# An early expert's list, gathers and weights: ranks moved ahead of the value products, all weight loads moved behind the gathers

## The chip, the cores and the metric

One core of one Trainium2 chip runs the whole program in one launch. The metric is the device time of one execution in microseconds (us), the median of three timed runs. One further execution was taken by the hardware profiler.

## The reference

The first stage is linear attention with a decay per head, for 4 batches, 8 heads, 768 positions and 64 columns a head; its output is the input of the second stage, a mixture of 8 experts in which each of the 3072 tokens goes to one expert.

```python
for b in range(nb):                               # blocks along the sequence
    intra = einsum(qb, kb) * Dmask                # decayed scores in the block
    out[:, :, sl] = intra @ vb + (qb * lam_pow) @ kv_state
    kv_state = lam_block * kv_state + (kb * rev_pow).T @ vb

x = out.transpose(0, 2, 1, 3).reshape(B * S, H * D)   # 3072 tokens x 512
logits = x @ w_gate                                    # 512 x 8
expert_idx = argmax(logits, axis=1)
gate_w = softmax(logits)[arange(N), expert_idx]
for e in range(8):
    mask = expert_idx == e
    out[mask] = gate_w[mask, None] * (maximum(x[mask] @ w1[e], 0) @ w2[e])   # 512->1024->512
```

## The kernel before

**Attention in steps.** The sequence is cut into six blocks of 128 positions (`n` = 0 to 5), and each block into two pairs of batches, which gives twelve steps. A step `i` of the loop works on three things at once: it makes the output rows and the router's logits of the step before (`leave`), it turns queries and keys of the step after (`enter`), and it computes the current step's state products (`attend_states`), the new state (`grow`) and the value products (`attend`). The scores of the next step (`score`) come last.

**Routing.** When the logits of a group of tokens are there, VectorE chooses each token's expert (`choose`). TensorE then computes the token's rank on its expert's list by products with triangular and full matrices of ones (`ranks`, tile `rank`), ScalarE copies it, and VectorE turns it into a place (`put`, tiles `place`, `slot`, `slot_i`). GpSimd writes one entry a token to that place in `slots`, in device memory, with an indirect DMA (`store_places`, line 467). The token rows themselves are stored to `xs` by ScalarE's queue (line 386).

**An early part of one expert.** Expert 5 (`FIRST`) does not wait for all tokens. Once the tokens of the first four blocks are placed (the group named `early`, ranked in loop step 8), the first 256 entries of its list are read (`start_early`, `list_0a`, line 497), its token rows are gathered on GpSimd (`gather_early`, tile `xg`, line 528), and its weights w1 and w2 (2 MB each) are loaded on SyncE's queue. After the last attention step TensorE turns the gathered rows (`tp`) and computes the hidden values (`ph`, line 607). For the output VectorE makes sums over w2 (`t_q`, `t_v`, `t_k`, `t_m`, line 684) and over the hidden values (`h_sd`, `h_qT`, `h_kT`, `h_kd`), from which seven products replace eight (line 775).

**Order.** `pin` keeps instructions of an engine in the order of the code; the rest is placed by a scheduler. A queue is worked off in order: an instruction that waits holds up what stands behind it on its engine. An explicit dependency (`add_manual_dep`, `hold`) makes one instruction wait for another's end. Before the change the first gather waits for the last scores of the step (`hold(begun[0], other)`), one half of w1 (by its rows) is loaded after the last attention inputs, the other half waits for the early list, and w2 waits for the gathers.

Of the kernel before, what the change touches and what calls it, by code (L numbers as in the profile page):

```python
# [22 lines left out]
def kernel(  # L23
# [207 lines left out]
    def pin(inst):  # L231
        tc.keep_in_program_order(inst)
        return inst
# [813 lines left out]
    def store_places(most, pin=pin):  # L1047
        put = None
        for k in range(min(most, len(waiting))):
            group, store, j = waiting.pop(0)  # L1050
            if k > 0:

                pin(nc.gpsimd.memset(between, 0.0))
            put = store(j)
            pin(put)
            if group[:2] == early and j == 1:
                start_early()
        return put

    def hold(inst, other):  # L1060
# [61 lines left out]
    def load_early():  # L1122

        w1t = wpool.tile([P, DC, F], F32, tag="w1", name="w1t")
        w2t = wpool.tile([P, FC, MD], F32, tag="w2", name="w2t")
        pin(nc.sync.dma_start(out=w1t[:, :DC // 2], in_=w1_r[FIRST][:, :DC // 2]))
        weights.append((w1t, w2t))

    def load_rest():

        rest = pin(nc.sync.dma_start(out=weights[0][0][:, DC // 2:], in_=w1_r[FIRST][:, DC // 2:]))
        tc.add_manual_dep(rest.ins, passes[0].read.ins.name, mybir.DependencyInfo(
            mybir.DependencyClass.Sync, mybir.DependencyReason.DATA),
            reason="the early list has the DMA engines first")

    def start_early():

        nc.vector.tensor_scalar(out=skip, in0=had, scalar1=-1.0, scalar2=float(EARLY),
                                op0=ALU.mult, op1=ALU.add)
        nc.vector.tensor_scalar_max(skip, skip, 0.0)  # L1140
        base[0] = const.tile([P, E], F32, name="ebase_late")
        nc.vector.tensor_copy(base[0], ebase)
        nc.vector.tensor_add(base[0][:, FIRST:FIRST + 1], base[0][:, FIRST:FIRST + 1], skip)
        passes.append(make_pass(FIRST, 0, EARLY, "0a", pin, nc.gpsimd))
        load_rest()

    def gather_early(other):

        m, w2t = passes[0], weights[0][1]
        pin(nc.gpsimd.memset(between, 0.0))  # L1150
        begun = fetch(m, 1 + (NSTEP - 2) * B * C, pin)
        hold(begun[0], other)
        behind = nc.sync.dma_start(out=w2t, in_=w2_r[FIRST])
        pin(behind)
        for other in begun:
            tc.add_manual_dep(behind.ins, other.ins.name, mybir.DependencyInfo(
                mybir.DependencyClass.Sync, mybir.DependencyReason.DATA),
                reason="the gathers have the DMA engines first")

    with tc.issue_after(keys_made.ins):  # L1160
        later_decays()
# [36 lines left out]
    fade(ahead)  # L1198
    last, cur = one, ahead

    for i in range(2, len(steps)):
        rest = leave(last, (4, 6, 7) if i < len(steps) - 1 else (4, 2, 3))

# [7 lines left out]
        if cur.n < NSTEP - 1:  # L1211
            attend_states(cur)
            grow(cur)
            attend(cur)
        else:
            attend(cur)
            attend_states(cur)
        to_sbuf(cur)
        if cur.n == NSTEP - 1:
            if ahead:  # L1220
                for s in range(2):
                    score(ahead, s)
                gather_early(ahead.scored)
            else:
                rest()
        update(cur)
# [6 lines left out]
        for group in ranked:  # L1233
            give_places(group)
        if ahead and i < len(steps) - 3:
            fade(ahead)
            store_places(1 if i < 5 else 2)
        last, cur = cur, ahead
    def turn_early():
        with tc.issue_after(decided[-1].ins):  # L1240
# [176 lines left out]
```

## Time and profile before

| | us |
|---|---|
| median of 3 timed runs | 433.21 (433.08 to 433.89) |
| the profiled execution's own time | 430.65 |
| its span | 428.9 |
| TensorE busy | 418.3 |
| VectorE, ScalarE, GpSimd busy | 263.5, 175.8, 256.8 |

The span is the time from the first to the last instruction in the trace; all times of day below are counted from its start. Busy time is time in which an engine works on an instruction; a wait that the profile names is idle time of an engine, put down to what ended it.

### The profile page before, as it was taken

To read this page: it belongs to the slowest core of one execution; us is meant where nothing else is said; L and a number is where in the kernel's file an instruction comes from. 1 tells how busy PE (TensorE), PEld (TensorE's weight loads), DVE (VectorE), ACT (ScalarE), POOL (GpSimd) and SP (SyncE) were. 2 spreads that over 40 slices of the span, in tenths; PEclk is the share of its full clock that TensorE was granted. 3 is DMA by queue.
4 is the path that set the end of the run, shared out by engine and by line. 5 is a ranking of instruction groups with operands and counts; after the bars stand their busy time and mean duration, and the time that the engine had idled before them with its cause. 6 is when DMAs were issued, how large, how long until landed. Compare 5 with 4: busy or idle time off the path is not lost. (4 is left out here: it accounts for less than half of the span.)

```text
span 428.9 us, 9593 instructions
## 1 busy us (share of the span) xinstructions
PE 418.3 (98%) x3707; PEld 393.1 (92%) x3707; DVE 263.5 (61%) x586; ACT 175.8 (41%) x318; POOL 256.8 (60%) x204
## 2 busy tenths in 40 slices
PE   8999999999999999999999999999999999999993
PEld 7878989888878897999999999999999999999973
DVE  7556646777567437686557657555565565765463
ACT  3365456556441434350654244345323605422221
POOL 4242556472444366977857848793884897749033
PEclk9999999999999999999999999999999999999998
DMA  9999999999985749975478746975975794753121
GB/s 173 209 247 239 210 245 237 229 228 222 284 287 165 224 93 272 282 262 213 64 162 224 281 74 150 311 200 126 292 240 79 218 373 74 156 188 55 21 82 63
DMA packets 164551, 83.11 MB, mean 194 GB/s; under 512 B 145923, under 2 KB 145959, under 8 KB 164496
## 3 DMA queue, kind: packets, MB, share of 16 engines
q1 hardware_dynamic: 155024, 63.21, 60.9%
q0 software_dynamic: 5536, 12.88, 9.4%
q10 hardware_dynamic: 3936, 6.31, 4.1%
q8 instruction: 31, 0.51, 0.5%
q14 instruction: 24, 0.20, 0.1%
HBM read 58.96 MB, written 12.72 MB: 167 GB/s over the span
## 5 line engine op out<-in xcount | busy, mean ns | idle before, releaser
L534 POOL DMA_INDIRECT out_dram<-o_room,list x24 | 26.3, 1097 | 53.3 <-DMA decay<-planes_q 29.4
L286 DVE TENSOR_TENSOR mt<-sp,decay 128x512 f32<-128x512 f32 x48 | 30.0, 684 | 19.8 <-PE sp L279 19.8
L740 ACT ACTIVATE hT<-hT 128x418 f32<-128x418 f32 (+6 forms) x56 | 28.1, 520 | 32.5 <-DVE hT L737 31.4
L729 PE MATMUL p<-xgT,w1t 128*128 128x209 f32 (+6 forms) x224 | 41.4, 327 | 0.0
L729 PEld LDWEIGHTS p<-xgT,w1t 128*128 128x128 f32 x224 | 37.1, 190 | 0.8 <-issue 0.8
L619 ACT COPY u_qT<-p 128x418 f32<-128x418 f32 (+6 forms) x14 | 6.7, 479 | 68.7 <-PE p L729 68.7
L915 PE MATMUL p<-hT,w2t 128*128 128x209 f32 (+5 forms) x192 | 33.6, 328 | 0.0
L915 PEld LDWEIGHTS p<-hT,w2t 128*128 128x128 f32 x192 | 32.0, 190 | 0.0
L528 POOL DMA_INDIRECT xg<-xs,list x25 | 26.1, 1044 | 9.1 <-issue 5.8
L467 POOL DMA_INDIRECT slots<-entry,slot_i x24 | 23.8, 990 | 12.2 <-PE tl L391 6.1
L737 DVE TENSOR_TENSOR hT<-p,u_kd 128x418 f32<-128x418 f32 (+6 forms) x28 | 15.6, 559 | 20.4 <-PE p L729 20.4
L279 PE MATMUL sp<-qT,kT 64*128 64x128 f32 x384 | 25.6, 280 | 0.6 <-DVE qs_room L255 0.6
L269 POOL TENSOR_TENSOR kd<-k_in,kdec 128x512 f32<-128x512 f32 x12 | 12.5, 1050 | 22.2 <-issue 10.7
L656 POOL TENSOR_TENSOR s_q<-w1t 128x1024 f32<-128x1024 f32 x7 | 16.5, 2361 | 14.9 <-DVE t_xT L714 12.9
L279 PEld LDWEIGHTS sp<-qT,kT 64*128 64x128 f32 x384 | 22.7, 188 | 2.8 <-issue 1.9
L607 PE MATMUL ph<-xgT,w1t 128*128 128x256 f32 (+1 forms) x128 | 21.6, 329 | 0.0
L326 ACT COPY xT<-op 128x512 f32<-128x512 f32 x12 | 7.0, 585 | 35.0 <-PE op L314 30.6
L586 ACT COPY xgT<-decay 128x1672 uint16<-128x1672 uint16 (+6 forms) x7 | 13.6, 1940 | 18.7 <-DMA decay<-planes_k 11.0
L607 PEld LDWEIGHTS ph<-xgT,w1t 128*128 128x128 f32 x128 | 19.3, 191 | 1.8 <-DVE xgT L598 0.3
L958 ACT ACTIVATE o_room<-o_room,list 128x512 f32<-128x512 f32 (+6 forms) x22 | 14.1, 709 | 16.1 <-DMA o_room<-qs_room 16.1
L729 PE MATMUL p<-t_sd,w1t 128*128 128x209 f32 (+6 forms) x112 | 20.7, 327 | 0.0
L729 PE MATMUL p<-st,s_q 128*128 128x209 f32 (+6 forms) x112 | 20.7, 327 | 0.0
(253 smaller groups left out, 1100.7 us busy)
## 6 DMA issues: line engine op xcount, KB each, us to landing
w2t<-in_moe_w_dram SPq DMA_DIRECT2D x8, 2048.0 KB, 9.4
w1t<-in_moe_w_dram SPq DMA_DIRECT2D x7, 2048.0 KB, 15.7
xs<-x_room ACTq DMA_DIRECT2D x12, 512.0 KB, 5.7
v_in<-in_v_dram SPq DMA_DIRECT2D x8, 512.0 KB, 8.8
o_room<-qs_room SPq DMA_DIRECT2D x76, 48.0 KB, 2.1
q_in<-in_q_dram SPq DMA_DIRECT2D x7, 512.0 KB, 8.8
k_in<-in_k_dram SPq DMA_DIRECT2D x7, 512.0 KB, 7.8
room<-in_q_dram SPq DMA_DIRECT2D x4, 512.0 KB, 9.1
```

The costliest lines, as they stand in the source:

```text
L279: m.scored = pin(nc.tensor.matmul(sp[u][:, i, b, :], lhsT=m.kT[s][halves[u], i, b, :], rhs=m.qT[s][halves[u], i, b, :], start=(i == 0 and ...
L286: nc.vector.tensor_mul(mt[:, u], sp[u], decay[:, u, s * HP // 2:(s + 1) * HP // 2].unsqueeze(2).to_broadcast(shp))
L467: put = nc.gpsimd.indirect_dma_start(out=slots, out_offset=bass.IndirectOffsetOnAxis(ap=slot_i[:, i:i + 1], axis=0), in_=entry[:, n, bs[i] ...
L528: return nc.gpsimd.indirect_dma_start(out=dst, out_offset=None, in_=xs[:rows, :], in_offset=bass.IndirectOffsetOnAxis(ap=idx, axis=0))
L534: put = nc.gpsimd.indirect_dma_start(out=out, out_offset=bass.IndirectOffsetOnAxis(ap=idx, axis=0), in_=src, in_offset=None, bounds_check= ...
L607: nc.tensor.matmul(ph, lhsT=w1t[:, dc, fc * P:(fc + 1) * P], rhs=m.xgT[:, dc, :], start=(dc == 0), stop=(dc == DC - 1))
L656: return nc.gpsimd.tensor_tensor(out=o, in0=x, in1=y, op=ALU.subtract)
L729: nc.tensor.matmul(p[:, i, :], lhsT=lhs[:, dc, g, i * P:(i + 1) * P], rhs=rhs[:, dc, :], start=(dc == 0), stop=(dc == DH - 1))
L737: lambda i, k, p, u: nc.vector.tensor_add(outs[i][k], p, u),
L740: pin(nc.scalar.activation(outs[i][k], outs[i][k], ACT.Relu))
L915: nc.tensor.matmul(p[:, c, :], lhsT=lhs[:, f, c * P:(c + 1) * P], rhs=rhs[:, f, :], start=(f == 0), stop=(f == FC // 2 - 1))
L958: pin(nc.scalar.activation(o_room[:w, t], o_room[:w, t], ACT.Copy, scale=gate))
```

## The change

The early group's ranks (on TensorE) and places (on VectorE) are issued in loop step 8 between `grow` and `attend`, and its two stores ahead of `fade`, the product `sd` on GpSimd; the list is read behind `fade`. The first gather no longer waits for the scores. The early part of w1 ahead of the list and its rest behind it are gone: w1, now in two column parts of 512 hidden columns each, and w2 are issued together, all three behind both gathers.

```diff
-            if group[:2] == early and j == 1:
-                start_early()
...
         w1t = wpool.tile([P, DC, F], F32, tag="w1", name="w1t")
         w2t = wpool.tile([P, FC, MD], F32, tag="w2", name="w2t")
-        pin(nc.sync.dma_start(out=w1t[:, :DC // 2], in_=w1_r[FIRST][:, :DC // 2]))
         weights.append((w1t, w2t))
-
-    def load_rest():
-
-        rest = pin(nc.sync.dma_start(out=weights[0][0][:, DC // 2:], in_=w1_r[FIRST][:, DC // 2:]))
-        tc.add_manual_dep(rest.ins, passes[0].read.ins.name, mybir.DependencyInfo(
-            mybir.DependencyClass.Sync, mybir.DependencyReason.DATA),
-            reason="the early list has the DMA engines first")
...
         passes.append(make_pass(FIRST, 0, EARLY, "0a", pin, nc.gpsimd))
-        load_rest()
-
-    def gather_early(other):
-
-        m, w2t = passes[0], weights[0][1]
+
+    def gather_early():
+
+        m, (w1t, w2t) = passes[0], weights[0]
         pin(nc.gpsimd.memset(between, 0.0))
         begun = fetch(m, 1 + (NSTEP - 2) * B * C, pin)
-        hold(begun[0], other)
-        behind = nc.sync.dma_start(out=w2t, in_=w2_r[FIRST])
-        pin(behind)
-        for other in begun:
-            tc.add_manual_dep(behind.ins, other.ins.name, mybir.DependencyInfo(
-                mybir.DependencyClass.Sync, mybir.DependencyReason.DATA),
-                reason="the gathers have the DMA engines first")
+        f = F // 2
+
+        for to, of in ((w1t[:, :, :f], w1_r[FIRST][:, :, :f]), (w1t[:, :, f:], w1_r[FIRST][:, :, f:]),
+                       (w2t, w2_r[FIRST])):
+            behind = pin(nc.sync.dma_start(out=to, in_=of))
+            for other in begun:
+                tc.add_manual_dep(behind.ins, other.ins.name, mybir.DependencyInfo(
+                    mybir.DependencyClass.Sync, mybir.DependencyReason.DATA),
+                    reason="the gathers have the DMA engines first")
...
         if cur.n < NSTEP - 1:
             attend_states(cur)
             grow(cur)
+            if chosen and chosen[-1][:2] == early:
+
+                for group in give_ranks():
+                    give_places(group)
+                last_early = i
             attend(cur)
...
-                gather_early(ahead.scored)
+                gather_early()
...
         if ahead and i < len(steps) - 3:
+            if i == last_early:
+                store_places(2)
             fade(ahead)
-            store_places(1 if i < 5 else 2)
+            if i == last_early:
+                start_early()
+            else:
+                store_places(1 if i < 5 else 2)
```

On TensorE, in loop step 8, before the change: the early group's ranks (`rank`) stand between the two halves of the next step's scores (`sp`).

```order
L279 MATMUL sp_1663<-qT,kT 128x128
L441 LDWEIGHTS before
L441 MATMUL rank<-oh,before 128x24
L441 LDWEIGHTS ones
L441 MATMUL rank<-so_far,ones 128x24
L441 LDWEIGHTS ones
L441 MATMUL rank<-oh,ones 128x16
L441 LDWEIGHTS ones
L441 MATMUL rank<-oh,ones 128x8
L279 MATMUL sp_1682<-qT,kT 128x128
```

And in the changed kernel, on TensorE in the same step: the ranks stand between the new state's products (`cp`) and the value products (`op`).

```order
L340 MATMUL cp<-room_68,kd 64x64 x16
L441 LDWEIGHTS before
L441 MATMUL rank<-oh,before 128x24
L441 LDWEIGHTS ones
L441 MATMUL rank<-so_far,ones 128x24
L441 LDWEIGHTS ones
L441 MATMUL rank<-oh,ones 128x16
L441 LDWEIGHTS ones
L441 MATMUL rank<-oh,ones 128x8
L314 MATMUL op_1605<-mt,room_68 64x128 x2
```

The same eight instructions moved up past the value products and half of the scores. VectorE follows: its places and `slot_i` stand ahead of the four `mt` products of that step instead of between and behind them.

On GpSimd, at the end of the same step (`kd` is the decayed keys of the step after, `sd` the faded state, `list_0a` the early list):

```order
 L269 TENSOR_TENSOR kd<-room_69,kdec 128x512
-L352 TENSOR_TENSOR sd<-st,sdec 128x512
-L467 DMA slots<-entry,slot_i 27648x4
-L1053 MEMSET between 128x1
-L467 DMA slots<-entry,slot_i 27648x4
+L467 DMA slots<-entry,slot_i 27648x4
+L1053 MEMSET between 128x1
+L467 DMA slots<-entry,slot_i 27648x4
+L352 TENSOR_TENSOR sd<-st,sdec 128x512
 L497 DMA list_0a<-slots 128x2x4
```

The two stores moved ahead of `sd`; the list read stays behind all three. Behind it stand, as before, two stores of the next group and then the two gathers.

On SyncE's queue, from the last attention inputs (`v_in`) to the first list of the later stage (`turns` is read for its expert):

```order
 L116 DMA v_in<-in_v_dram 128x16x64 x2
-L1126 DMA w1t<-in_moe_w_dram 128x2x1024
-L1131 DMA w1t<-in_moe_w_dram 128x2x1024
-L1153 DMA w2t<-in_moe_w_dram 128x8x512
-L1289 TENSOR_LOAD turns
+L1145 DMA w1t<-in_moe_w_dram 128x4x512 x2
+L1145 DMA w2t<-in_moe_w_dram 128x8x512
+L1291 TENSOR_LOAD turns
```

There are three loads of the same bytes in the same places of the queue; what each waits for and which part of w1 it brings is different.

## Rows read from the trace of the kernel before

**Rows 1.** The page's first line, and its line of busy times (us, share of the span, instructions).

```profile
span 428.9 us, 9593 instructions
PE 418.3 (98%) x3707; PEld 393.1 (92%) x3707; DVE 263.5 (61%) x586; ACT 175.8 (41%) x318; POOL 256.8 (60%) x204
```

**Rows 2.** All waits of TensorE between 85 and 165 us: who waited for whom, us in total, times, longest.

```profile
PE p L783 <- DVE u_t L820: 0.4, 1, 0.4
PE tx L376 <- ACT xT L326: 0.3, 1, 0.3
```

**Rows 3.** Timelines of TensorE and VectorE around the early part of the expert: start, duration, engine, line, operation, out<-in, count, in brackets idle time before it and what ended it.

```profile
122.07 2.00 PE L607 MATMUL ph<-xgT,w1t 128*128 128x256 f32 x8
139.63 1.89 PE L775 MATMUL p<-t_k,h_kT 128*128 128x256 f32 x8
...
131.16 1.23 DVE L684 TENSOR_TENSOR t_q<-w2t 128x1024 f32<-128x1024 f32 x1 [3.50 <-DMA w2t<-in_moe_w_dram]
136.79 0.69 DVE L754 TENSOR_TENSOR h_qT<-hT 128x512 f32<-128x512 f32 x1 [0.27 <-ACT hT L560]
137.52 0.69 DVE L755 TENSOR_TENSOR h_kT<-h_qT,hT 128x512 f32<-128x512 f32 x1
```

**Rows 4.** Timeline of TensorE: the scores and the logits behind them in a step without ranks, and in the step with the early group's ranks between the halves of the scores.

```profile
73.56 2.06 PE L279 MATMUL sp<-qT,kT 64*128 64x128 f32 x32
75.54 0.64 PE L366 MATMUL lgT<-xT,gates 128*32 128x256 f32 x8
...
92.89 1.16 PE L279 MATMUL sp<-qT,kT 64*128 64x128 f32 x16
...
95.27 0.64 PE L366 MATMUL lgT<-xT,gates 128*32 128x256 f32 x8
```

**Rows 5.** Timeline of VectorE: state updates (`st`), `mt` products and the two `slot_i` in question, the early group's and the next group's.

```profile
91.33 0.69 DVE L362 TENSOR_TENSOR st<-cp,sd 128x512 f32<-128x512 f32 x1 [0.24 <-PE cp L340]
94.09 1.29 DVE L286 TENSOR_TENSOR mt<-sp,decay 128x512 f32<-128x512 f32 x2 [2.06 <-PE sp L279]
...
98.01 0.16 DVE L465 CAST slot_i<-slot 128x2 int32<-128x2 f32 x1
...
101.12 0.69 DVE L362 TENSOR_TENSOR st<-cp,sd 128x512 f32<-128x512 f32 x1
...
106.95 0.17 DVE L465 CAST slot_i<-slot 128x2 int32<-128x2 f32 x1
```

**Rows 6.** Timeline of GpSimd: `sd`, the early group's two stores, the list read and the two gathers.

```profile
95.33 1.04 POOL L352 TENSOR_TENSOR sd<-st,sdec 128x512 f32<-128x512 f32 x1
98.45 1.00 POOL L467 DMA_INDIRECT slots<-entry,slot_i  x1 [2.08 <-DVE lg L393]
...
99.76 0.96 POOL L467 DMA_INDIRECT slots<-entry,slot_i  x1 [0.19 <-issue]
107.11 0.78 POOL L497 DMA_DIRECT2D list_0a<-slots  x1 [6.39 <-DMA slots<-entry,slot_i]
...
113.89 1.00 POOL L528 DMA_INDIRECT xg<-xs,list_0a  x1 [3.31 <-PE rank L441]
115.19 0.97 POOL L528 DMA_INDIRECT xg<-xs,list_0a  x1 [0.30 <-issue]
```

**Rows 7.** Timeline of SyncE's queue: the rest of w1 and w2 of the early expert, and a later expert's w2 and w1.

```profile
111.52 0.37 SPq L1131 DMA_DIRECT2D w1t<-in_moe_w_dram  x1
119.75 0.37 SPq L1153 DMA_DIRECT2D w2t<-in_moe_w_dram  x1
...
184.16 0.38 SPq L204 DMA_DIRECT2D w2t<-in_moe_w_dram  x1
184.79 0.37 SPq L202 DMA_DIRECT2D w1t<-in_moe_w_dram  x1
```

**Rows 8.** Issue to landing of transfers. First two lines of the page (count, size of each, median us to landing): the two halves of the early w1, and the row stores. Then the landing lines of the views of one tile: w1 between 95 and 140 us (two halves and the next expert's 2 MB), w2 in the same stretch (one load), w1 between 180 and 205 us (one load, that issued at 184.79).

```profile
w1t<-in_moe_w_dram SPq DMA_DIRECT2D x2, 1024.0 KB, 6.7
xs<-x_room ACTq DMA_DIRECT2D x12, 512.0 KB, 5.7
DMA to landing us min/median/max: 6.7/8.0/9.2
DMA to landing us min/median/max: 11.3/11.3/11.3
DMA to landing us min/median/max: 13.7/13.7/13.7
```

**Rows 9.** Stretches of two microseconds: length, busy time of TensorE, its weight loads, VectorE, ScalarE, GpSimd (instructions), granted clock, busy share of the DMA engines, GB/s moved.

```profile
122.00:124.00 2.00, 1.98 (x13) 1.63 (x13) 1.68 (x13) 0.85 (x3) 1.48 (x3) 1.00 0.95 334
124.00:126.00 2.00, 2.00 (x14) 1.80 (x12) 1.84 (x18) 0.56 (x2) 1.80 (x4) 1.00 0.94 251
126.00:128.00 2.00, 2.00 (x11) 1.74 (x11) 1.45 (x9) 0.64 (x2) 1.50 (x2) 1.00 1.05 407
```

**Rows 10.** The rows of the expert behind the early one: the last transpose for `decay` on SyncE's queue, the page's line of such transposes (median us to landing), ScalarE's copy that joins them, and TensorE's wait for `u_t`.

```profile
152.04 1.19 SPq L578 DMA_TRANSPOSE decay<-planes_k  x1
decay<-planes_k SPq DMA_TRANSPOSE x11, 3.5
156.09 2.09 ACT L586 COPY xgT<-decay 128x1672 uint16<-128x1672 uint16 x1 [7.72 <-PE ph L607]
163.03 1.08 PE L783 MATMUL p<-w2t,qs_room 128*64 128x256 f32 x8 [0.36 <-DVE u_t L820]
```

More of the change, by code (lines that the diff above doesn't have):

```diff
@@ L1199 @@
     last, cur = one, ahead
+    last_early = None
     for i in range(2, len(steps)):
```

## Prediction

> **What bounds the kernel now.** I read the page's first lines, then the waits of TensorE, then the timelines of every engine between 88 and 165 us, and last the transfers. TensorE is busy 418.3 of the 428.9 us, and almost none of what is left is waiting: between 85 and 165 us, where the whole change lies, it waits 0.4 us for VectorE's `u_t` and 0.3 us for ScalarE's `xT` [rows 1, 2]. So the reader should see two things. An earlier list, gather or weight can take away a wait of TensorE only if there is one, and there is 0.7 us of it. A later weight can make a new one without limit. The question is therefore how much slack each moved thing had, and how much it keeps.
>
> The slack before. The early hidden products start at 122.07, and the first half of w1 and its rest are there by then. The sums over w2 start on VectorE the moment w2 lands, at 131.16; VectorE has 0.27 us of rest before `h_qT`, and `h_kT`, finished at 138.21, is read by TensorE at 139.63, 1.42 us later [rows 3]. So w2 may land 0.27 + 1.42 = 1.7 us later, at 132.8, before TensorE notices.
>
> **The change part by part.**
>
> *The early ranks go ahead of the step's value products.* They are the same four products on TensorE. Between two halves of the scores they cost something: from the scores to the logits it is 75.54 - 73.56 = 1.98 us without ranks, and 95.27 - 92.89 = 2.38 us with them, 0.40 us [rows 4]. Their new place, between two other groups, may cost as much (gain 0) or nothing (gain 0.4). I take a gain of 0.2 us. The products they need from VectorE (`oh`) are ready before the state update at 91.33, so they wait for nothing new.
>
> *VectorE computes the places ahead of the `mt` products.* `slot_i` was ready at 98.17, behind them. Now the chain starts behind the update that ends at 92.0, in the 2.06 us in which VectorE was idle until 94.09; four to five small operations of about 0.2 us put `slot_i` at about 93.2 [rows 5]. The cost on the path is nothing: that idle time hides it, and were it too short, `mt` would be some tenths late, with TensorE reading it a whole set of products later.
>
> *On GpSimd the two stores pass the `sd` product.* The first takes the start of `sd`, about 95.5 instead of 98.45, the second 96.8 instead of 99.76. `sd` (1.04 us) comes 2.6 us later and ends near 99; its reader, the next state update, stands at 101.12, so this costs nothing with 2 us of cover, and beyond them one for one [rows 5, 6]. The list read waited for the second store until 107.11, 7.35 us after that store's start; the same wait now gives 104.2. The list then lands 4.4 us later, as before between 107.11 and the load at 111.52 that waited for it: 108.6 [rows 6, 7].
>
> *The gathers are no longer held for the scores.* They were released at 113.89. What stands ahead of them now is the pair of stores of the next group, whose `slot_i` is made at 106.95 to 107.12 and does not move. Stores and gathers follow each other at 1.3 us: stores at 107.3 and 108.6, gathers at 109.9 and 111.2 instead of 113.89 and 115.19 [rows 5, 6]. The list (108.6) is there. So the gathers gain 4.0 us, not the whole lead of the list. Behind them on GpSimd stand stores that wait for later ranks anyway.
>
> *All of w1 and w2 wait for both gathers.* The load of w2 was issued 119.75 - 115.19 = 4.56 us after the second gather started [rows 6, 7]; so the three loads are now issued at 111.2 + 4.6 = 115.8. For w2 that is 4 us earlier; for the rest of w1 (111.52) it is 4.3 us later, and for its early part far later still. Behind them in SyncE's queue stand only the lists of the later experts, which wait for the last routing anyway, so it is the weights alone that wait.
>
> First column part, 1 MB: the rest of w1, also 1 MB and also beside half a megabyte of other traffic, took 6.7 us to land; 115.8 + 6.7 = 122.5 against the use at 122.07, a stall of 0.4 us [rows 3, 8]. Bounds: no stall if the gathers land half a microsecond sooner, and with the 9.2 us of the slowest w1 load in that stretch 125.0, a stall of 2.9 us. The Trainium skill ("DMA: Bandwidth & Descriptors", section on the anatomy of one DMA on the gpsimd path) fits a transfer by about 2.0 us plus its bytes over 436 GB/s. An estimate from it is 4.4 us for this part, which would land at 120.2 and stall nothing, and the sum would end at 433.0. This case's trace does not agree: 6.7 us for 1 MB, 11.3 us for 2 MB.
>
> Second column part: first needed by the fifth of eight hidden blocks; the row at 122.07 is one block, 2.00 us, so four of them hide it for 7 to 8 us, more than the whole 6.7 us of such a load [rows 3, 8].
>
> w2 is now last of 4 MB in one queue. Lower bound: the pair w2 and w1 of a later expert, issued at 184.16 and 184.79, had landed 13.7 us after the second issue, 14.3 us after the first: 115.8 + 14.3 = 130.1. Upper bound: twice the 11.3 us that w2 took here, 22.6 us: 138.4, a stall of 5.6 us [rows 7, 8]. In between: 4.2 MB of weights and two row stores of 0.52 MB are 5.2 MB; at the mean of 122 to 128, (334 + 251 + 407) / 3 = 331 GB/s, that is 15.8 us, landing at 131.6 [rows 8, 9]. I take 131.6, nearer the pair because the bytes lie behind each other in one queue as they do there: about when it lands today, with 1.2 us of slack left.
>
> **Sum.** -0.2 (ranks) + 0.4 (first part of w1) + 0 (w2, places, `sd`, second part) = +0.2 us. The profiled execution took 430.65 us, 428.9 of span and 1.75 around it; 430.9 after. The median of the timed runs, 433.21, is 2.56 us above the profiled one; with the same difference, 433.4 us. A measurement of this kernel can tell about 0.2% (0.87 us) from no change, so this is no change.
>
> **Rivals.**
>
> *Slower: the weights are late.* The point from which it decides is w2 at 133.7 or the first part of w1 at 122.9. For it: the rate between 124 and 126 is only 251 GB/s [rows 9], and both slacks left are near one microsecond. Against it: the later pair, which landed in 14.3 us [rows 7, 8]. Landing one to two microseconds past these points costs as much: 434.4 to 435.4; at the upper bound of w2 438.8.
>
> *The early stores land no earlier, so the change doesn't do what it says.* If the list read stays at 107.11 because the input loads, not the store's start, set its landing, the list lands at 111.5, the gathers start at 111.6 and 112.9, the loads at 117.5, w1's first part lands at 124.2: stall 2.1 us, 435.1. For it: the second store took 7.35 us although it moves 2 KB [rows 6].
>
> *The later lists are late.* The last stores run beside w2. The transposes of the next expert's rows, last one for `decay` issued at 152.04, must land before 156.09, where ScalarE's join stands behind TensorE; at 3.5 us from issue to landing they have 0.5 us of slack, and what comes later reaches TensorE through `u_t`, where it waits already (0.36 us) [rows 10]. Two microseconds late gives 434.7. Against it: the DMA engines carry the same bytes by 130 us as before.
>
> *Faster.* All of it must come together: 0.4 us from the ranks and both waits of 0.7 us gone, 1.1 us in all, 432.1. For it: w2 may land 1 us sooner, and the list chain with it. Against it: neither wait is for a transfer or a list directly [rows 2].
>
> **How the numbers follow.** Forecast (-0.4 to +0.8 us about no change) 0.56; weights late 0.17; stores no earlier 0.07; lists late 0.06; faster 0.14. Predicted is the forecast's 433.4. From the cases: faster 0.14, same 0.56, slower 0.30. The range leaves out half of "faster" below 432.3 and the tail of the late weights above 435.3.
>
> **What would show it.** Right: the list read near 104, the gathers at 109.9 and 111.2, three loads issued near 115.8; TensorE's first hidden product delayed by under a microsecond with the load as its releaser; VectorE's sums over w2 starting between 130 and 133; the waits of TensorE between 85 and 165 us between 0.5 and 1.5 us in total. Wrong: a wait of TensorE for w1 or `t_k` of more than a microsecond, a list read still at 107, or a stretch in which TensorE, never idle, is shorter than before by more than the 0.4 us of the ranks.

## The result, and the profile after

The changed kernel takes 436.10 us (median of 10 runs, 435.18 to 438.87), the kernel before 433.12 on the same chip (10 runs, 432.22 to 433.89). The ratio is 1.0071, with an interval of 1.0053 to 1.0089: about 3 us slower, past the upper end of the predicted range (435.3).

One thing must be known to read the numbers below: executions of one kernel differ by chip and from one to the next. On the chip of this result the kernel before stays within 432.2 to 433.9; on the chips 6, 7, 9 and 13 of the experiments its executions spread from 430.4 to 438.2. Its trace shown ahead of the prediction (430.65) is one of the short ones, 2.5 us below its median and 1.6 us below the shortest of these ten executions; the changed kernel's (436.38) lies at its median. So of the 5.6 us between the two spans only some 3 can belong to the change. The medians below are of all executions, while a ratio and its interval leave out those that fell into a slower state, so a ratio need not be the quotient of the medians beside it.

The changed kernel's first lines of the page, as [rows 1]:

```profile
span 434.5 us, 9595 instructions
PE 419.9 (97%) x3707; PEld 392.3 (90%) x3707; DVE 266.6 (61%) x586; ACT 176.2 (41%) x318; POOL 256.4 (59%) x204
```

Its waits of TensorE from 85 to 165 us, as [rows 2] (who waited for whom, us in total, times, longest):

```profile
PE lgT L366 <- issue: 1.1, 1, 1.1
PE op L305 <- issue: 1.0, 3, 0.4
PE tx L376 <- ACT xT L326: 0.3, 1, 0.3
PE ph L607 <- ACT hT L560: 0.2, 1, 0.2
```

No wait for a weight, a list or a gather stands there. What is new is 2.1 us in which TensorE was idle for nothing that the profile names ("issue"). The products around these gaps are stretched as well: from the first state product to the scores behind them it is 3.4 us here (112.58 to 115.95) and 1.0 us in the trace of before (110.49 to 111.52). The moved steps, from the timelines of GpSimd, SyncE's queue, VectorE and TensorE, as [rows 3, 5 to 7]:

```profile
103.71 0.81 POOL L497 DMA_DIRECT2D list_0a<-slots  x1 [4.49 <-DMA slots<-entry,slot_i]
...
112.08 1.00 POOL L528 DMA_INDIRECT xg<-xs,list_0a  x1 [0.19 <-issue]
113.38 0.97 POOL L528 DMA_INDIRECT xg<-xs,list_0a  x1 [0.30 <-issue]
...
117.39 1.49 SPq L1145 DMA_DIRECT2D w1t<-in_moe_w_dram  x2
118.93 0.50 SPq L1145 DMA_DIRECT2D w2t<-in_moe_w_dram  x1
...
109.04 0.17 DVE L465 CAST slot_i<-slot 128x2 int32<-128x2 f32 x1
...
126.50 1.99 PE L607 MATMUL ph<-xgT,w1t 128*128 128x256 f32 x8
```

The list read came at 103.7, as forecast. The gathers came 2.2 us later than forecast because the next group's `slot_i` was made at 109.04 instead of 106.95: TensorE was already 2 us late in that step. By the first hidden product (126.50 instead of 122.07) it was 4.4 us late, late enough for w1 to be there. This trace alone would lead to a wrong reading; the experiments start from that.

### The profile page after: what moved, and what is told of

Read it like the earlier page. It is cut to its first block, busy times and chain, and to the rows that moved or that the text cites. A ratio compares the mean times of both kernels' runs of the same rounds, so it can differ in the third digit from the quotient of the medians.

```text
span 434.5 us, 9595 instructions
## 1 busy us (share of the span) xinstructions
PE 419.9 (97%) x3707; PEld 392.3 (90%) x3707; DVE 266.6 (61%) x586; ACT 176.2 (41%) x318; POOL 256.4 (59%) x204
## 4 chain that ended last, share of the span: by engine, by line
PE 87%; DMA 2%; SPq 2%; DVE 2%; issue 2%; ACT 2%; another core or an unknown queue 1%; POOL 0%; POOLq 0%; ACTq 0%
PE p L729 29%; PE p L915 26%; PE sp L279 5%; PE op L314 4%; PE p L775 4%; PE tx L376 3%; PE op L305 3%; PE cp L340 2%; PE tk L241 2%; PE ph L607 2%; PE tq L241 2%; PE lgT L366 2%; PE p L783 2%; SPq L578 1%; DMA gates<-in_moe_w_gate_dram 1%
## 5 line engine op out<-in xcount | busy, mean ns | idle before, releaser
L729 PE MATMUL p<-t_xT,w1t 128*128 128x209 f32 (+6 forms) x112 | 20.6, 326 | 0.0
L653 POOL TENSOR_TENSOR w1t<-w1t 128x1024 f32<-128x1024 f32 x7 | 20.2, 2892 | 0.6
```

What stands on the lines that cost most here:

```text
L653: return nc.gpsimd.tensor_tensor(out=o, in0=x, in1=y, op=ALU.add)
L729: nc.tensor.matmul(p[:, i, :], lhsT=lhs[:, dc, g, i * P:(i + 1) * P], rhs=rhs[:, dc, :], start=(dc == 0), stop=(dc == DH - 1))
```

## Experiments

"Ratio" is to the kernel before on the same chip in the same series, with its 95% interval. A `...` in an edit marks lines left out.

**The change taken apart.** Four kernels on chip 9, kernel before 434.14 us. They were to tell three theories apart that the first trace left: the earlier gathers slow TensorE beside them, the ranks' new place costs, or the loads do.

*Only the ranks, places, stores and list moved* (the hunks on these alone; hold and loads as before):

```diff
...
+            if chosen and chosen[-1][:2] == early:
+                for group in give_ranks():
+                    give_places(group)
+                last_early = i
             attend(cur)
...
```

> The kernel before with only the early ranks, places, stores and list read moved as in the change; the hold of the gathers and the loads of w1 and w2 stay as before. Theory 1 (gathers beside short products): no change, 432.9 to 433.3. Theory 2 (ranks and stores): 1 to 1.5 us slower, 434.1 to 434.6, with a gap ahead of the logits of step 8. Theory 3 (weights): no change.

> The kernel with only the early ranks, places, stores and list moved, once more. In its first trace moving the ranks gained 0.28 us at the scores and lost 0.29 us ahead of the value products, so the time should be that of the kernel before, ratio 0.997 to 1.002; the first time it was 0.9982. A gain of more than 0.3% would need a cause that its trace doesn't show.

Measured: 431.82 us, 0.9982 [0.9946, 1.0019], and later 431.56, 0.9975 [0.9934, 1.0016]. The ranks' new place costs what the old one did: logits 1.98 us behind the scores instead of 2.38, and the value products 0.31 us later than in the kernel before, at 91.36 instead of 91.05:

```profile
91.36 1.97 PE L314 MATMUL op<-mt,room 128*64 128x128 f32 x32
93.26 2.06 PE L279 MATMUL sp<-qT,kT 64*128 64x128 f32 x32
95.24 0.64 PE L366 MATMUL lgT<-xT,gates 128*32 128x256 f32 x8
```

This part doesn't slow the kernel.

*Only the hold taken from the gathers:*

```diff
-        hold(begun[0], other)
```

> The kernel before with one thing taken out: the first early gather no longer waits for the scores of its step. Theory 1, gathers beside the short state products and scores slow TensorE (in the changed kernel's trace the state products of loop step 10, 112.58 to 115.95, hold gaps of 0.28, 0.29 and 0.44 us while GpSimd issues its gathers from 112.08 to 114.35): about 2 us slower, 435 us, with such gaps beside the gathers at about 111.6 and 112.9. Theory 2, the early ranks, places and stores cost (the logits of step 8 come 1.4 us later in the changed kernel's trace): no change, 433.1. Theory 3, the late weights cost: no change, 433.1.

Measured: 435.41 us, 1.0023 [0.9981, 1.0065]. Its trace has no gaps; but there the gathers begin just behind the state products, so it doesn't settle their part (the second trace of the changed kernel does, below: gathers from 110.08, state products from 110.41, no gap). What this execution lost it lost in a wait of TensorE for GpSimd:

```profile
PE p L729 <- POOL s_q L656: 3.0, 1, 3.0
```

*Both together, the loads as before:*

> The whole change except the loads: early ranks and stores, gathers not held, but w1 in two row halves and w2 loaded as before. Theory 1: 2 to 3 us slower, about the changed kernel's 436. Theory 2: 1 to 1.5 us slower. Theory 3 (the loads of the weights make the difference): no change, 433.1. Sum of 1 and 2: 436 or more.

Measured: 434.86 us, 0.9989 [0.9942, 1.0037] (its edit is the two above together): all of the change without its loads is no slower than the kernel before.

*Only the loads changed, ranks and hold as before:*

```diff
-        pin(nc.sync.dma_start(out=w1t[:, :DC // 2], in_=w1_r[FIRST][:, :DC // 2]))
...
+        for to, of in ((w1t[:, :, :f], w1_r[FIRST][:, :, :f]), (w1t[:, :, f:], w1_r[FIRST][:, :, f:]),
+                       (w2t, w2_r[FIRST])):
+            behind = pin(nc.sync.dma_start(out=to, in_=of))
...
```

> The kernel before with only the loads changed: all of w1 in two column parts and w2 behind the gathers, which stay held for the scores. Here the loads are issued near 119.8 and the first part of w1 lands 6.7 us later, 126.5, against its use at 122.07: if that working is right, a wait of TensorE of about 4 us at the first hidden product, 437 us. If the load lands in 4.4 us, 2 us slower. Theories 1 and 2 alone say no change.

Measured: 441.62 us (six executions, 436.05 to 444.62), 1.0111 [1.0043, 1.018]. The loads were issued at 120.75, and TensorE waited for them:

```profile
126.23 2.59 PE L607 MATMUL ph<-xgT,w1t 128*128 128x256 f32 x8 [3.11 <-DMA w1t<-in_moe_w_dram]
```

So on this chip the loss is the loads'. That the earlier gathers, which the rest of the change gives, take part of it back is argued only: the loads are issued at 120.75 here and at 116.35 in the changed kernel's second trace, but the intervals of the two ratios (below for the changed kernel) overlap. The first part let TensorE go 5.5 us after its issue here, sooner than the 6.7 us of the forecast.

**The changed kernel again, and with one load moved back.** Chip 7, kernel before 432.45 us.

> The changed kernel once more, unaltered, so that its second trace can be laid beside its first. In the first, TensorE lost 1.2 us ahead of the logits at 97 us and 2.3 us inside the state products at 112 to 116 us, before any of the moved weights had been issued, and nothing at the hidden products. Theory W (the weights are late): those two gaps are chance and don't come again; TensorE is on time at 122 and waits there for the first part of w1, by 117.4 + 6.7 = 124.1 about 2 us or more; the time is again 2 to 4 us above the kernel before. Theory G (the gaps belong to the change): they come again at the same products, over 1 us each, and there is no wait for w1. Theory L (the later list): neither, but TensorE waits more than 1 us for s_q of line 656 near 165 us.

Measured: 435.09 us, 1.0066 [1.0032, 1.01]. The gaps are gone and the wait is there. GpSimd, SyncE's queue, TensorE, VectorE:

```profile
104.22 0.81 POOL L497 DMA_DIRECT2D list_0a<-slots  x1 [5.34 <-DMA slots<-entry,slot_i]
...
110.08 1.00 POOL L528 DMA_INDIRECT xg<-xs,list_0a  x1 [0.36 <-DVE new L420]
111.38 0.97 POOL L528 DMA_INDIRECT xg<-xs,list_0a  x1 [0.31 <-issue]
...
116.35 0.99 SPq L1145 DMA_DIRECT2D w1t<-in_moe_w_dram  x2
117.39 0.74 SPq L1145 DMA_DIRECT2D w2t<-in_moe_w_dram  x1
...
124.25 3.65 PE L607 MATMUL ph<-xgT,w1t 128*128 128x256 f32 x8 [2.27 <-DMA w1t<-in_moe_w_dram]
...
134.65 1.23 DVE L684 TENSOR_TENSOR t_q<-w2t 128x1024 f32<-128x1024 f32 x1 [3.15 <-DMA w2t<-in_moe_w_dram]
```

TensorE is let go 7.9 us after the load's issue, having waited 2.27 us, and its first hidden block then takes 3.65 us where it took 2.00 [rows 3]. The stretches of this trace, as [rows 9], tell why: the granted clock falls from 1.00 to 0.57, near the lower of its two levels (1.2 of 2.4 GHz), right behind the idle time:

```profile
120.00:122.00 2.00, 1.98 (x25) 1.61 (x17) 1.40 (x6) 1.36 (x5) 0.00 (x0) 1.00 1.07 415
122.00:124.00 2.00, 0.00 (x0) 0.00 (x0) 1.74 (x12) 0.78 (x3) 1.54 (x3) 1.00 1.03 382
124.00:126.00 2.00, 1.75 (x4) 1.45 (x5) 0.07 (x1) 0.00 (x0) 0.65 (x2) 0.58 1.01 341
126.00:128.00 2.00, 2.00 (x10) 1.42 (x9) 0.00 (x0) 0.00 (x1) 0.00 (x0) 0.57 1.05 404
128.00:130.00 2.00, 2.00 (x10) 1.77 (x11) 1.86 (x17) 0.70 (x3) 1.07 (x2) 1.00 1.15 248
```

The wait and the slow block are 2.27 + 1.65 = 3.9 us; the span is 432.9, 4.0 above that of the kernel before.

*The first column part of w1 loaded where the kernel before loaded its first half*, the rest as in the changed kernel:

```diff
+        pin(nc.sync.dma_start(out=w1t[:, :, :F // 2], in_=w1_r[FIRST][:, :, :F // 2]))
         weights.append((w1t, w2t))
...
-        for to, of in ((w1t[:, :, :f], w1_r[FIRST][:, :, :f]), (w1t[:, :, f:], w1_r[FIRST][:, :, f:]),
+        for to, of in ((w1t[:, :, f:], w1_r[FIRST][:, :, f:]),
                        (w2t, w2_r[FIRST])):
```

> The changed kernel, with the first column part of w1 loaded where the kernel before loaded its first half, after the last attention inputs, instead of behind the gathers; the second part and w2 stay behind the gathers. Theory W: the wait for the first part is gone, the second part is covered by four hidden blocks, and the time is that of the kernel before, within 0.3% (ratio 0.997 to 1.003). Theories G and L: the load changes nothing at the places they name, and the time stays 2 us or more above the kernel before (ratio 1.005 or more).

> The kernel with the first column part early, once more, beside the next one, to see if either beats the kernel before. In its first trace w2 landed at 131.8 and TensorE lost nothing at the change's places; its only loss was 3.0 us for s_q near 165, as other kernels have it in some executions. Expected ratio to the kernel before 0.996 to 1.001. If moving the ranks is worth 0.4 us (0.1%), it can't be told from 1.

> The kernel with the first column part of w1 early, a third time. Theory W on either kind of chip: ratio 0.995 to 1.002 to the kernel before, no wait for w1. Theory K on a chip with gaps: the gaps stay, since only the load is moved back, and the ratio is 1.005 or more.

> The kernel with the first column part of w1 early, a fourth time. Ratio to the kernel before 0.994 to 1.000, after 0.9977, 0.9976 and 0.9951. On a chip with gaps: if they belong to the chip and the program's length or order, they stand here too and the kernel before has its own; if they belong to the late load, they are gone.

Measured on the chips 7, 9, 6 and 13: 431.38 us, 0.9977 [0.9938, 1.0017]; 432.49, 0.9976 [0.9929, 1.0023]; 431.79, 0.9951 [0.9914, 0.9988]; 433.33, 1.0004 [0.9955, 1.0052]. In none of the four traces does TensorE wait for a weight. On chip 7, side by side, one load moved back takes 3.7 us from the changed kernel. There this version is faster than the changed kernel, and on none of the four chips is it shown to be slower than the kernel before; that it beats that one too (mean of the four ratios 0.9977) only one interval says. Its row of the hidden products, from the second trace:

```profile
121.95 1.99 PE L607 MATMUL ph<-xgT,w1t 128*128 128x256 f32 x8
```

*The first part behind the list* (one load added to `start_early`, waiting for `passes[0].read`, and taken from `gather_early`):

> The changed kernel with the first column part of w1 behind the early list, where the kernel before had its rest, instead of behind the gathers; the second part and w2 stay behind the gathers. The list is read at 102 to 104 us and lands some 3 to 4 us later, so this part is issued near 107 to 108.6 and lands by 118. Theory W (only the lateness of the first part costs): no wait for w1 at 122, and the time is that of the kernel before or 0.3% below, ratio 0.995 to 1.002. Rival (the transfer holds up the gathers, which then hold up the rest): gathers land later, the second part and w2 are issued a microsecond or more later, w2 lands past 133, and the time is 1 to 3 us above.

Measured on chip 9: 435.01 us, 1.002 [0.9977, 1.0063]. No wait for w1, as expected; the ratio lies at the upper end of what was expected and its interval doesn't tell it from 1. VectorE's sums over w2 start at 132.51, 1.6 us later than in the second trace of the kernel above, so of the rival the later landing of w2 is seen, though not past 133.

**Why the first part is late.** The changed kernel, with the second part and w2 waiting for the first part:

```diff
...
+            if len(begun) == 2:
+                begun.append(behind)
```

> The changed kernel, with the second part of w1 and w2 waiting for the first part, which so has the queue to itself. In the changed kernel it was issued at 116.35 and let TensorE go at 124.25, 7.9 us later, and moved beside the two other loads. Theory S (it is late because the others share the engines): it lands 2 us sooner, near 122, TensorE waits 0.5 us or less there and the clock stays up; but w2 is issued near 122 and lands 11 to 13 us later, at 133 to 135, which leaves TensorE a wait of up to 2 us for the sums over w2 near 140; the time is 1 to 2 us below the changed kernel's or the same. Theory P (its place alone): it lands at 124 as before, the others come 7 us later still, TensorE waits for the second part or for the sums over w2 by 4 us or more, and the time is 438 or more.

Measured on chip 12: 438.09 us, 1.0117 [1.0085, 1.0149], beside 437.06 for the changed kernel.

```profile
120.09 5.25 SPq L1145 DMA_DIRECT2D w1t<-in_moe_w_dram  x2
125.39 0.56 SPq L1145 DMA_DIRECT2D w2t<-in_moe_w_dram  x1
```

The two issues of the first row lie 4.9 us apart, since the second waits for the first's landing: with nothing behind it in its queue the part lands in 4.9 us, not 7.9. That alone doesn't show that the loads behind it make it late, for the chip and the time within the step differ too. The table has every 1 MB load of w1 in the traces that had nothing left ahead of it in its queue and whose end a trace shows. "Took" is the time from issue to landing, or until TensorE is let go or the waiting load is issued; "beside it" is what the queues of GpSimd and ScalarE moved in that time.

| load | issued at | behind it in its queue | beside it | took |
|---|---|---|---|---|
| first part alone (this kernel) | 120.09 | nothing | 0.26 MB | 4.9 us |
| rest of w1, kernel before with the sums ahead (below) | 112.98 | nothing | 0.34 MB | 5.4 us |
| rest of w1, only the hold taken | 111.84 | nothing | 0.46 MB | 6.0 us |
| rest of w1, kernel before | 111.52 | nothing | 0.56 MB | 6.7 us |
| first part, behind the list | 108.35 | nothing | 0.81 MB | 7.7 us |
| rest of w1, the change without its loads | 113.57 | nothing | 1.34 MB | 8.1 us |
| second part, first part behind the list | 118.29 | 2 MB | 0.03 MB | 5.1 us |
| first part, only the loads changed | 120.75 | 3 MB | 0.06 MB | 5.5 us |
| second part, first part early (chip 6) | 116.31 | 2 MB | 0.52 MB | 7.7 us |
| first part, with products of zeros (chip 9, below) | 117.47 | 3 MB | 0.52 MB | 7.7 us |
| first part, changed kernel (second trace) | 116.35 | 3 MB | 0.52 MB | 7.9 us |

Some of the lines behind the table: the page's lines of the two loads with the first part behind the list, as seen from 107 to 110 and from 117 to 120 us (count, size, us to landing); ScalarE's queue, by which the row stores go (packets, MB, share), while the first part was on its way in the changed kernel's second trace and in the kernel with only the loads changed; and the row store of that second trace.

```profile
w1t<-in_moe_w_dram SPq DMA_DIRECT2D x1, 1024.0 KB, 7.7
w1t<-in_moe_w_dram SPq DMA_DIRECT2D x1, 1024.0 KB, 5.1
...
q10 hardware_dynamic: 272, 0.52, 30.8%
q10 hardware_dynamic: 40, 0.06, 3.0%
...
116.04 0.37 ACTq L386 DMA_DIRECT2D xs<-x_room  x1
```

The loads behind don't make a load late by themselves: 5.1 and 5.5 us with 2 and 3 MB behind it. In both groups the time grows with what the other queues move beside the load; in the changed kernel's second trace that is a row store, issued 0.3 us ahead of the part. At half a megabyte beside it, a load took 6.0 and 6.7 us with nothing behind it, and 7.7 to 7.9 with 2 or 3 MB behind it. So theory S fits only together with the row store, and the table alone doesn't tell cause from effect, since a load that takes longer also meets more traffic. No run moves the row store by itself, and on the chip where the loads behind were held back no trace shows when the part lands in the unaltered kernel.

The median is 1 us above the changed kernel's, with intervals that overlap. The trace shows no wait of TensorE for the second part or for the sums over w2; TensorE is 2.6 us later than in the changed kernel's trace from this chip (below) already at the early ranks, 94.47 instead of 91.83, ahead of all these loads.

**The clock.** Ten products of zeros ahead of the early hidden products, to keep TensorE busy while it waits:

```diff
+            if fc == 0 and m is passes[0]:
+                for r in range(10):
+                    nc.tensor.matmul(ph[:, :P], lhsT=zeros, rhs=zeros, start=True, stop=True)
```

> The changed kernel with ten products of a tile of zeros (0.22 us each) on TensorE ahead of the early hidden products: two ahead of the last logits, eight ahead of the last ranks. They change no value. In the second trace of the changed kernel TensorE waited 2.27 us for w1 until 124.25, and the next eight hidden products took 3.65 us where they took 2.00 before; the granted clock from 124 to 128 was 0.57. Theory C (the wait costs twice, since the clock falls to its lower level behind it): with TensorE busy until about 124 the clock stays at 1.00, the hidden products take 2.00 us again, and the time is 1 to 2 us below the changed kernel's, about 433.5 to 434.5. Rival (the slower products have another cause, as the transfers beside them): they take 3.6 us again, and the time is that of the changed kernel or 0.4 us above it, 435 to 436.

Measured on chip 9: 435.00 us, 1.0037 [1.0001, 1.0074]. In the trace the wait is 0.23 us, and all 8 hidden blocks take 14.08 us:

```profile
125.21 14.08 PE L610 MATMUL ph<-xgT,w1t 128*128 128x256 f32 x64 [0.23 <-DMA w1t<-in_moe_w_dram]
```

The granted clock stays at 1.00 in the stretches in question:

```profile
124.00:126.00 2.00, 1.77 (x16) 1.58 (x15) 1.90 (x18) 0.17 (x1) 1.62 (x5) 1.00 1.01 326
126.00:128.00 2.00, 2.00 (x11) 1.77 (x10) 1.79 (x11) 0.38 (x1) 1.81 (x3) 1.00 1.02 373
```

The trace bears out that idle time brings the lower clock; the ratio is lower than the changed kernel's, but the intervals overlap. So both on one chip, 12, kernel before 433.40:

> The changed kernel, unaltered, beside the filled one on the same chip. Expected: ratio to the kernel before 1.004 to 1.009, as in its first two series (1.0071 and 1.0066), and in its trace either a wait for w1 of about 2 us near 122 with the granted clock below 0.7 behind it, or gaps ahead of it of the same size.

> The changed kernel with ten products of zeros ahead of the early hidden products, once more, beside the changed kernel itself. If the fallen clock costs 1.6 us in the timed executions too, its median is 1 to 2 us below that of the changed kernel on this chip. If the two medians agree within 0.5 us, the clock's share, seen in the trace, is not the part that the timed executions lose, or is taken up by the products of zeros.

Measured: 437.06, 1.0084 [1.0066, 1.0102], and 438.88, 1.013 [1.0114, 1.0146]. Here the products cost 1.8 us instead of saving any. On this chip the gaps of the first trace are back, at the same products, TensorE reaches the first hidden product at 128.1, and neither trace has a wait for w1 to fill. State products in the changed kernel's third trace, on chip 12:

```profile
112.63 0.90 PE L305 MATMUL op<-qs_room,st 64*64 64x128 f32 x10
113.83 0.46 PE L305 MATMUL op<-qs_room,st 64*64 64x128 f32 x4 [0.30 <-issue]
114.58 0.27 PE L305 MATMUL op<-qs_room,st 64*64 64x128 f32 x1 [0.29 <-issue]
115.31 1.21 PE L305 MATMUL op<-qs_room,st 64*64 64x128 f32 x17 [0.46 <-issue]
```

The same in its second trace, on chip 7:

```profile
110.41 1.10 PE L305 MATMUL op<-qs_room,st 64*64 64x128 f32 x32
```

The two spans of chip 12 are alike, 435.5 and 435.4, because the first lost elsewhere much of what the products of zeros (0.61 + 1.95 us) cost the second. Behind its gaps, none longer than 0.5 us, the granted clock fell to 0.50, and the scores that follow took 3.17 us; with the products of zeros the gaps are there too, the clock stayed at 1.00, and they took 2.06. Both rows of the scores, and the stretches of the changed kernel's third trace:

```profile
116.45 3.17 PE L279 MATMUL sp<-qT,kT 64*128 64x128 f32 x32
115.81 2.06 PE L279 MATMUL sp<-qT,kT 64*128 64x128 f32 x32
...
116.00:118.00 2.00, 2.00 (x23) 1.67 (x18) 0.00 (x0) 1.07 (x2) 0.00 (x0) 0.50 0.35 135
118.00:120.00 2.00, 2.00 (x28) 1.88 (x27) 1.45 (x3) 0.17 (x1) 0.00 (x0) 0.79 0.67 188
```

So a trace shows what the clock costs on chip 7 and on chip 12. The timed executions don't settle it: of the changed kernel's six on chip 12 the three with a mean granted clock of 0.993 took 437.4 to 438.0 us and the three with 0.996 or 0.997 took 436.1 to 436.7, but on chip 7 two with 0.997 and 0.998 took 434.7 and 434.9, in the midst of the seven from 0.990 to 0.992 (434.2 to 436.5).

**The later list.** In several traces, with and without the changed loads, TensorE waits 0.5 to 3.0 us for `s_q`, which GpSimd computes behind the gathers of a later list. The sums put ahead of these gathers, in both kernels:

```diff
...
             w1, finish = first_sums(weights[i][0])
+            if i == 1:
+                finish(None)
...
```

> The changed kernel, with the sums s_q and s_v of the second expert's w1 (line 656, GpSimd) ahead of the third expert's gathers, and no longer waiting for VectorE's sums. GpSimd was idle there from 153 to 158 us in the kernel before, so they need no room, and TensorE's products over s_q near 165 us no longer depend on when the third expert's list lands. Theory L: the whole loss of the change goes, and the time is that of the kernel before with the same sums, within 0.3%. Theory W: it is 2 us or more above that kernel, as the change is above the kernel before.

> The kernel before with the same sums ahead of the gathers. In its profiled run s_q ended 0.08 us ahead of TensorE's use; in two variants TensorE waited 1.9 to 3.2 us there. If that wait is what spreads the executions from 430.4 to 438.1 us, the median falls by 1.5 to 3 us to about 431 to 432.5 (ratio 0.993 to 0.997) and the spread narrows to some 3 us; if it is not, the time is the same within 0.2%, since nothing else is taken away.

Measured on chip 7: 435.34 us, 1.0075 [1.0044, 1.0106], and 432.65, 1.0004 [0.9963, 1.0045]. The wait for `s_q` is gone and nothing is won: VectorE's sums, now beside GpSimd's, take 1.98 us instead of the 0.42 of the kernel before, and TensorE waits for them. VectorE's timeline of the kernel before with the sums moved:

```profile
156.21 1.98 DVE L754 TENSOR_TENSOR qs_room<-hT 128x256 f32<-128x256 f32 x1
```

And of TensorE's waits in the same trace:

```profile
PE p L784 <- DVE qs_room L754: 1.3, 1, 1.3
```

The loss of the change stays as it was, so it isn't the later list's. In the changed kernel's trace of this pair there is no wait for w1 either: after a wait of 0.9 us for an input TensorE reached the first hidden product at 122.90, and the first part, issued at 115.94, was there, 7.0 us later at most. It then lost 0.7 us to the sums over w2, as said below.

**The kernel before, traced once more**, for the gaps:

> The kernel before, for a second trace. On a chip where its executions lie between 432.2 and 434 us without any near 430.6: theory H (the gaps belong to the chip) expects gaps of 1 to 2.5 us in total at single instructions of TensorE, with no releaser, that the first trace lacks; theory K (they belong to the change) expects a trace like the first, 430 to 431 us, or a loss near 16 or 165 us only. On a chip with executions near 430.6 both expect a trace like the first.

Measured on chip 6: 432.39 us, 0.9985 [0.9933, 1.0038] to itself, a chip with short executions and a trace without the gaps. Inconclusive.

## Why the prediction was wrong

**What bounds the kernel** was right as far as the chips 7 and 9 show: the moved ranks and the earlier list and gathers bring nothing (ratio 0.9989 without the loads), and what was left was a new wait. On the chip of the result no trace shows that wait.

**Ranks, places, stores, list, gathers.** The ranks were to gain 0.2 and gain nothing: 0.4 at the scores, 0.3 given back ahead of the value products. List read 103.7 and 104.2 (forecast 104.2), gathers at 110.08 and 111.38 in the second trace (109.9 and 111.2). The rival of stores that land no earlier is refuted. Loads issued at 116.35 (115.8): 5.0 us behind the second gather instead of 4.6.

**The first column part is the step that failed**, as far as the traces show. Its term was 6.7 us, a landing at 122.5 and a stall of 0.4. In the changed kernel's second trace it took 7.9, and TensorE waited 2.27 us, until 124.25: 0.55 us of that comes from the later issue, 1.2 from the longer landing, 0.1 from TensorE being early. The row that I took, the rest of w1, had half a megabyte of other traffic beside it, as the prediction says, and so had the part; but the part had 3 MB behind it in its queue too, and the row had nothing. That fits the 1.2 us (6.0 and 6.7 against 7.7 to 7.9 in the table), but it isn't shown: the run that holds these loads back has half as much traffic beside the part, and without the other traffic the part took 5.5 us with the same 3 MB behind it. Loads of this size took 4.9 to 8.1 us, and the prediction let the part be only 0.4 us later than its sum before it would count as late. The upper bound, 9.2 us, held by luck: I read it as the slowest load of a part, but it is the next expert's load of 2 MB, issued at 133.6. The Trainium skill's fit ("DMA: Bandwidth & Descriptors", section on the anatomy of one DMA on the gpsimd path), an estimate of 4.4 us, comes near the loads with the least traffic beside them (4.9 to 5.5 us) and is far from the 7.9; the page gives it for DMAs on GpSimd's path, and these are SyncE's.

**The price of a stall was the second failure.** I counted it one for one. The 2.27 us cost 1.65 us more in the slow block (and the 3.1 us of the loads' kernel 1.6 us more in its hidden products, 15.9 us from their first to their last instead of 14.3), a cost no row of before could show, since TensorE was never idle so long there between 85 and 165 us; it would have put the upper bound of 2.9 us above 4.

**Second part and w2.** The second part was hidden, as said. w2 was 3 us later than the 131.6 forecast: `t_q` at 134.65 and 135.08, past the 132.8 from which TensorE would notice. In the second trace 1.6 us of this is the later issue (117.39) and 1.5 the time to landing, 17.3 us instead of 15.8. It notices nothing in these traces only because it is 3.8 us and more late itself; with 0.9 us of delay from an input, in the trace with the sums ahead, it waited 0.7 us for `h_kT`. So with the first part in time, all of the prediction's slack for w2 would have been spent in the changed kernel, for a wait of some 1.5 us (an estimate: the 0.7 us, and the 0.8 us by which TensorE was late there); with that part loaded early w2 lands in time (`t_q` at 130.93 in the second trace).

**Rivals.** "The weights are late" is what happened on the chips 7 and 9, at the place named (w1's first part past 122.9), and 0.17 was too little for it: it had two chances to come true, and in the second trace both points were crossed. Its price, 434.4 to 435.4, lacked the clock. The later lists are no part of the loss.

**What stays open.** The wait for w1 is shown in one trace of the changed kernel, on chip 7, and in the traces with only the loads changed and with products of zeros, on chip 9. With the sums ahead, also on chip 7, the profiled execution has no such wait, yet the ratio of that kernel is alike, 1.0075. On the chip of the result and on chip 12 TensorE is late by then from gaps at fixed products, and no wait for a weight is seen, yet the ratios are alike, 1.0071 and 1.0084. Whether the kernel before has such gaps there (it is 2 us above its best there), and whether the early first part helps there, no run shows: all four of its runs fell on other chips. What releases TensorE in the gaps, no view names. So that the late first part makes the 3 us of the result is not shown; shown is that the loads make the loss on chip 9 and that moving one of them back takes it away on chip 7.

## What to carry to other kernels

A load moved behind a chain lands by its new issue time plus what it takes beside the other transfers of that moment, in its own queue and in the others, and 1 MB took 4.9 to 8.1 us here. So look up what moves then, take the slow row of a view, make sure that it is of a load of the same size, and load what is read first earlier. A wait of two microseconds on TensorE cost nearly twice itself in one trace (2.27 and 1.65 us), so add what the granted clock may take behind it. And take a second trace before explaining a difference: here the first one showed another loss than the second, at the same ratio.

## What the runs showed of the hardware

After the 2.27 us wait that ended at 124.25 the granted clock was 0.58 and 0.57 for some 4 us; after the 3.1 us of the loads' kernel it was down to 0.50 from 128 to 130; on chip 12 it was 0.50 from 116 to 118 behind state products that were broken by three gaps of 0.3 to 0.5 us (112.63 to 116.45). Loads of 1 MB took 4.9 to 5.5 us with up to 0.34 MB moved beside them by other queues, even with 2 or 3 MB behind them in their own; with half a megabyte beside them they took 6.0 and 6.7 us with nothing behind them and 7.7 to 7.9 us with 2 or 3 MB behind them. VectorE's sums of 128x256 took 0.42 us with GpSimd idle and 1.98 beside GpSimd's sums of 128x1024. And gaps of 0.3 to 1.1 us recur at the same instructions in every trace of the changed kernel and its variants from two chips, and in none from four others.
